# Attention with top-k, then an exact-GELU MLP: one attention item normalised inside the next item's search, and the MLP begun one slot earlier

## The chip, the cores and the metric

The kernel runs on one core of one Trainium2 chip. The metric is the device time of one execution in microseconds (us), the median of several runs. The core's engines are called PE (matrix products; PEld is its loading of weights), DVE (vector), ACT (activation functions and copies), POOL (GpSimd) and SP (which issues DMAs here). Each executes its own list of instructions in order, and they wait for each other by semaphores.

## The reference

```python
# q, k, v: (8, 8, 576, 64) float32; w_in: (512, 2048), w_out: (2048, 512), both handed over as float64
scores = scale * np.matmul(q, k.transpose(0, 1, 3, 2))
kth = np.partition(scores, -32, axis=-1)[..., -32:-31]
scores = np.where(scores >= kth, scores, -1e9)
scores = scores - np.max(scores, axis=-1, keepdims=True)
attn = np.exp(scores)
attn = attn / (np.sum(attn, axis=-1, keepdims=True) + 1e-09)
o = np.matmul(attn, v).astype(np.float32)
x = o.transpose(0, 2, 1, 3).reshape(4608, 512)
h = x @ w_in
g = 0.5 * h * (1.0 + erf(h / sqrt(2)))
out = (g @ w_out).astype(np.float32)
```

For each query the 32 largest of 576 scores are kept, the softmax is taken over them, the result multiplies v, and the rows of all heads together are the 4608 tokens of an MLP with 2048 hidden features.

## The kernel before, in words

**Items and slots.** Two heads of one batch are a pair. An item is 128 query rows of both heads of a pair, so a score tile is 128 partitions by 2 x 576. There are 144 items (a batch of 576 rows has four full row tiles per pair; the last 64 rows of two pairs share one item). The order of the items is made in the list `items`: in batch 0, items 0 to 7 are row tiles 0 and 1 of the pairs 0 to 3, items 8 to 15 are row tiles 2 and 3 of these pairs, 16 and 17 are the remainders. The scheduling is manual: the order in which the Python program issues instructions is the order in each engine's list. The main loop (L616) runs over slots n. In one slot, item n+2 gets its scores (`scores`, PE and ACT), item n its search for the 32 largest (`top_k`, DVE: four rounds of two MAX8 with three rounds of two MATCH_REPLACE8 between them, L323 and L326), item n-1 its softmax (`softmax`, ACT: a steep Prelu against the threshold at L362, and an Exp that also sums, L363), item n-2 its transposes (`transposes`: the PE transposes at L394 and L412, and ACT's copies from PSUM into the tile pt at L395 and L419), and item n-3 its product with v (`attend`, only when n-3 is the second item of a pair of row tiles: 20 PE rows at L443 for both, and a copy into xT at L448).

**Normalising.** After the softmax of item n-1, POOL adds 1e-9 to its sums (`add_small`, L355). DVE takes the reciprocal (`inverse`, L349); in `top_k` a dictionary of hooks says after which round it is issued, and before the change this is always round 3, the end of the search. Then `normalise` (L375) multiplies the two halves of the item, on DVE or POOL: with on_dve = 0 both on POOL, 1 one on each, 2 both on DVE. L660 picks this from the weight unit that the next slot will convert, since conversion keeps POOL busy. `threshold` makes the negated threshold and maximum on POOL (L338, L341) from the search's result.

**Weights.** The float64 weights are loaded as 16-bit words and converted to float32 in 16 units, one to a slot: slots 1 to 15 and 17, in the order given by `ORDER`. ACT does two steps of a unit (L174, L176) and, up to the slot before START, a third one (L178, an unsigned conversion); from slot START on the third step is POOL's (L190) and `on_pool` says so. POOL adds the parts at L193 and L194 (`weights_add`).

**The MLP** is cut into pieces in one list, `pieces`. A piece of the first layer (l1, L495) is two matmuls of 128x256 for full row tiles; a piece of the second layer (l2, L531) is one of 128x512. Eight make a block: two l1 blocks come first, then l2 and l1 blocks alternate. Two gelus (L506) on ACT are issued behind the first block, and behind the sixth piece of each l2 block. Gelu and Exp lie in different tables of ACT, so a table is loaded each time ACT turns from one to the other. A slot issues up to `left[0]` pieces spread between its attention work: 8, or 7 in the seven slots after START. A piece is issued only when its tokens are there: `attend` raises `n_tok` when a row tile is complete over all four pairs. The first 256 tokens are complete with item 7's product, the next 256 with item 15's, which is issued in slot 18. After START (`late`) the second half of the softmax is issued behind the first transposes rather than directly behind the first half. START is 2 * NP + 2 = 10 with NP = 4 pairs.

**PSUM.** The tiles of tag "tp" (q/k transposes, the scores' tail t_ps, the transposes of an item, the product o) take turns in two buffers, so each waits until ACT has copied out the tile two before it. The l1 results have two buffers of their own (tag "l1").

**SP** issues the loads of q, k, v, the weights and the stores of the output, in program order.

Of the kernel before, what the change touches and what calls it, by code (L numbers as in the profile page):

```python
# [14 lines left out]
def kernel(  # L15
# [19 lines left out]
    nc = tc.nc  # L35
# [3 lines left out]
    ALU = mybir.AluOpType  # L39
# [6 lines left out]
    NP = H // 2  # L46
# [74 lines left out]

    ORDER = [0, 1, 2, 3, 8, 9, 4, 5, 10, 11, 6, 7, 12, 13, 14, 15]
    FIRST = 1
    START = 2 * NP + 2
    WARM = 16
    words = {}
    low = const.tile([P, 1], f32, name="low")
# [52 lines left out]
    def on_pool(u):  # L180

        return SLOT_OF[u] >= START

# [23 lines left out]
    def place_of(b, row):  # L207

        if row < SM:
            return b // 2 * RING + b % 2 * (SM + 2 * TL) + row  # L210
        return b // 2 * RING + SM + b % 2 * TL + row - SM

    N = len(items)
# [30 lines left out]
    S_of, stat_of = {}, {}  # L244

    def row(i, e):
        return S_of[i][:, e * S : (e + 1) * S]
# [10 lines left out]
    def halves(t, e, step):  # L258

        return spread(t[:, e * TL :], step + (TL if e == 0 else -TL), TL)  # L260
# [47 lines left out]
    def top_k(i, hooks):  # L308


        stat_of[i] = st = {
            "top": work.tile([P, 2, TOPK], f32, tag="top", name="top"),
            "neg": work.tile([P, 2, 2], f32, tag="neg", name="neg"),
            "bias": work.tile([P, 2], f32, tag="bias", name="bias"),
            "den": work.tile([P, 2], f32, tag="den", name="den"),
            "rden": work.tile([P, 2], f32, tag="rden", name="rden"),
        }
        cur = [row(i, e) for e in range(2)]
        rest = work.tile([P, 2, S], f32, tag="rest", bufs=1, name="rest")
        n_op = 0  # L320
        for r in range(TOPK // 8):
            for e in range(2):
                nc.vector.max(st["top"][:, e, 8 * r : 8 * r + 8], cur[e])  # L323
            if r < TOPK // 8 - 1:
                for e in range(2):
                    nc.vector.match_replace(  # L326
                        rest[:, e], st["top"][:, e, 8 * r : 8 * r + 8], cur[e], LOWEST
                    )
                cur = [rest[:, e] for e in range(2)]
            if r in hooks:  # L330
                hooks.pop(r)()
# [13 lines left out]
    def inverse(i):  # L345
        if i < 0 or i >= N:
            return
        st = stat_of[i]
        nc.vector.reciprocal(st["rden"], st["den"])  # L349

    def add_small(i):
        if i < 0 or i >= N:
            return
        st = stat_of[i]
        nc.gpsimd.tensor_scalar(st["den"], st["den"], 1e-9, None, op0=ALU.add)  # L355
# [12 lines left out]
    def normalise(i, on_dve):  # L368

        if i < 0 or i >= N:  # L370
            return
        st = stat_of[i]
        for e in range(2):
            s = row(i, e)
            (nc.vector if e >= 2 - on_dve else nc.gpsimd).tensor_scalar(  # L375
                s, s, st["rden"][:, e : e + 1], None, op0=ALU.mult
            )
# [5 lines left out]
    def transposes(i):  # L383

        if i < 0 or i >= N:
            return []
        t, s = items[i][1], S_of.pop(i)

        def tails():
            tp = ps.tile([P, 512], f32, tag="tp", name="tp_t")  # L390
            if t < NM:
                if t % 2 == 0:
                    pt_now[0] = work.tile([P, 2 * NM + 1, 2 * P], f32, tag="pt", name="pt")
                nc.tensor.transpose(tp[:, 0:P], s[:, SM : S + TL], ident)  # L394
                nc.scalar.copy(out=pt_now[0][:, 2 * NM, t % 2 * P : (t % 2 + 1) * P], in_=tp[:, 0:P])  # L395
            else:
                pt_now[0] = ptt
                for r in range(2):
                    nc.tensor.transpose(
                        tp[0:TL, r * P : (r + 1) * P], s[:, r * S + SM : (r + 1) * S], ident  # L400
                    )
                for e in range(2):
                    c = slice(e * TL, (e + 1) * TL)
                    nc.scalar.copy(
                        out=halves(ptt[c, 0, NM, :], e, NJ * P), in_=halves(tp[0:TL, 0 : 2 * P], e, P)
                    )

        def main(e):
            tp = ps.tile([P, 512], f32, tag="tp", name="tp")
            first = e * (S + TL if t < NM else S)  # L410
            for j in range(NM):
                nc.tensor.transpose(  # L412
                    tp[:, j * P : (j + 1) * P], s[:, first + j * P : first + (j + 1) * P], ident
                )
            if t < NM:
                dst = pt_now[0][:, e * NM : (e + 1) * NM, t % 2 * P : (t % 2 + 1) * P]
            else:
                dst = ptt[:, e, 0:NM, :]
            nc.scalar.copy(out=dst, in_=tp.rearrange("p (j n) -> p j n", j=NM))  # L419

        return [tails] + [lambda e=e: main(e) for e in range(2)]
# [3 lines left out]
    def attend(i):  # L425

        if i < 0 or i >= N:
            return False
        pair, t = items[i]
        b, at = divmod(pair, NP)  # L430
        if t < NM and t % 2 == 0:
            return False
        pt = pt_now[0]
        o = ps.tile([P, 512], f32, tag="tp", name="o")
        n, row = (2 * P, (t - 1) * P) if t < NM else (TL, SM)
        tok = place_of(b, row)
        assert read[0] >= tok + n - RING
        c = slice(tok % RING, tok % RING + n)
        if t < NM:
            vt = raw_of("v", pair)  # L440
            for j in range(NJ):
                for e in range(2):
                    nc.tensor.matmul(  # L443
                        o[e * D : (e + 1) * D, 0:n], lhsT=vt[:, j, e, :],
                        rhs=pt[:, e * NM + j if j < NM else 2 * NM, :],
                        start=(j == 0), stop=(j == NJ - 1),
                    )
            nc.scalar.copy(out=xT[:, at, c], in_=o[:, 0:n])  # L448
        else:
            for r in range(2):  # L450
                vt = raw_of("v", pair + r)
                for j in range(NJ):
                    for e in range(2):
                        nc.tensor.matmul(  # L454
                            o[e * D : (e + 1) * D, r * TL : (r + 1) * TL], lhsT=vt[:, j, e, :],
                            rhs=pt[:, r, j, half(r, e)], start=(j == 0), stop=(j == NJ - 1),
                        )
            nc.scalar.copy(
                out=xT[:, at : at + 2, c],
                in_=o[:, 0 : 2 * TL].rearrange("p (r n) -> p r n", r=2),  # L460
            )

        if t == (NM if b % 2 == 0 else NM - 1):
            for r in range(2 if t == NM else 1):
                load("v", pair + r + NP + 1)
        if at == (NP - 1 if t < NM else NP - 2):
            assert n_tok[0] == tok
            n_tok[0] = tok + n
        return True
# [146 lines left out]
    for n in range(ahead):  # L616

        left[0] = 7 if START < n < START + 2 * NP else 8
        weights_add(unit_in(n))
        scores(n + 2)  # L620
        product = attend(n - 3)
        late = n > START
        mlp(1)
        tr = transposes(n - 2)
        if product and n > START and done[0] < len(pieces) and pieces[done[0]][0] > ready[0]:

            for piece in tr[:1]:
                piece()
            tr, ready[0] = tr[1:], n_tok[0]
        softmax(n - 1, 0)  # L630
        mlp(1)
        if not late:
            softmax(n - 1, 1)
        mlp(1)
        prep = prep_in.pop(n, [])
        if len(prep) > 1 and len(tr) == 3:
            tr, prep = tr[:1] + prep[:1] + tr[1:], prep[1:]
        for piece in tr[:-1]:
            piece()
            ready[0] = n_tok[0]  # L640
            mlp(1)
        ready[0] = n_tok[0]
        if late:
            softmax(n - 1, 1)
        add_small(n - 1)
        for piece in tr[-1:] + prep:
            piece()
            mlp(1)

        run_gelus()  # L650
        mlp(left[0])
        run_gelus()
        if n < N:
            top_k(n, {3: lambda: inverse(n - 1)})
        else:
            inverse(n - 1)
        threshold(n)
        u = unit_in(n + 1)

        normalise(n - 1, 0 if u not in words else 2 if on_pool(u) else 1)  # L660

        weights_size(unit_in(n + 1))
        if n >= FIRST:
            load_weights(n + 2)
        if n <= NP:
            load("v", n)
# [38 lines left out]
```

## Time and profile before

| | |
|---|---|
| median of 5 runs | 1655.5 us (1654.88 to 1658.2) |
| profiled execution, its own time | 1658.2 us |
| its span | 1656.4 us |
| PE busy | 1596.7 us (96%) |
| DVE busy | 1419.7 us (86%) |
| ACT busy | 1185.1 us (72%) |
| POOL busy | 651.6 us (39%) |

The span is the time from the first to the last instruction that the profile records; the run's own time has 1.8 us more. Time in the profile is counted from the span's start. DVE begins the search of slot 8 at 94.72 us, of slot 9 at 105.06, of slot 10 at 115.83 and of slot 18 at 210.89; the last search ends before 1603. A row of the profile in order of time gives the start, the length, the engine, the line, the operation with the tile that it writes and those that it reads, how many such instructions follow on each other, and in brackets how long the engine had been idle and what ended that. The count of PE rows is of hardware matmuls: a float32 matmul of the program is two. "PEclk" is the granted clock of PE as a share of full speed.

### The profile page before, as it was taken

The numbers are of one execution on the slowest core, as the hardware profiler recorded it, in microseconds if no ns is written. First come the engines' busy times: TensorE is split into PE (matmuls) and PEld (weight loads), VectorE is DVE, ScalarE is ACT, GpSimd is POOL, SyncE is SP. The second block draws the span as 40 slices with busy tenths as digits, with TensorE's granted clock in tenths as the row PEclk, the third lists the DMA queues.
The fourth block names the chain that finished last, engine by engine and source line by source line (L and its number), as shares of the span: only waits on it lengthen the run. The fifth ranks groups of instructions, "written<-read, shape, count | busy, mean of one in ns | idle before, by whom it ended". The sixth has DMA issues, their size and how long they took to land.

```text
span 1656.4 us, 25056 instructions
## 1 busy us (share of the span) xinstructions
PE 1596.7 (96%) x8832; PEld 1081.4 (65%) x8832; DVE 1419.7 (86%) x3049; ACT 1185.1 (72%) x2131; POOL 651.6 (39%) x756
## 2 busy tenths in 40 slices
PE   6669899999999999999999999999999999999999
PEld 4446566766666667676666667676666666666665
DVE  7998889999999898998999888998889898999800
ACT  6888767777777777777777777777777777777720
POOL 3677643333333333333333333333333333333300
PEclk7669999999999999999999999999999999999999
DMA  6423210011100111011110111001110001000000
GB/s 165 138 99 98 87 42 1 14 29 29 49 1 22 32 30 31 1 28 36 29 28 1 42 29 43 1 14 28 44 35 1 27 15 32 4 14 3 5 13 13
DMA packets 126621, 56.14 MB, mean 34 GB/s; under 512 B 117760, under 2 KB 117792, under 8 KB 126496
## 3 DMA queue, kind: packets, MB, share of 16 engines
q1 hardware_dynamic: 125376, 54.25, 12.2%
q8 instruction: 70, 1.15, 0.3%
q14 instruction: 55, 0.45, 0.1%
q10 hardware_dynamic: 1056, 0.26, 0.1%
q0 software_dynamic: 64, 0.03, 0.0%
HBM read 45.08 MB, written 9.44 MB: 33 GB/s over the span
## 4 chain that ended last, share of the span: by engine, by line
PE 90%; DVE 6%; ACT 3%; POOL 0%; issue 0%; ACTq 0%; DVEq 0%; POOLq 0%
PE h_ps L495 30%; PE y_ps L531 30%; PE o L443 8%; PE s_ps L276 7%; PE tp L412 7%; DVE top L323 3%; DVE rest L326 2%; PE tp_qk L231 2%; PE t_ps L272 2%; PE o L454 1%; PE s_ps L297 1%; PE tp_t L394 1%; ACT s L363 1%; ACT s L362 1%; POOL s L375 0%; PE warm L595 0%
## 5 line engine op out<-in xcount | busy, mean ns | idle before, releaser
L323 DVE MAX8 top<-rest 128x8 f32<-128x576 f32 x864 | 610.1, 748 | 0.0
L495 PE MATMUL h_ps<-xT,w_in_sb 128*128 128x256 f32 (+1 forms) x2560 | 554.8, 362 | 3.8 <-ACT g L506 3.8
L531 PE MATMUL y_ps<-w_out_sb,g 128*128 128x512 f32 x1152 | 549.4, 599 | 0.0
L495 PEld LDWEIGHTS h_ps<-xT,w_in_sb 128*128 128x128 f32 x2560 | 429.4, 191 | 67.1 <-issue 19.6
L375 POOL TENSOR_SCALAR s<-s,rden 128x576 f32<-128x576 f32 x266 | 456.6, 1726 | 0.8 <-issue 0.4
L326 DVE MATCH_REPLACE8 rest<-top,rest 128x576 f32<-128x576 f32 x576 | 423.8, 744 | 0.0
L355 POOL TENSOR_SCALAR den<-den 128x2 f32<-128x2 f32 x144 | 32.1, 223 | 837.6 <-ACT s L363 837.1
L531 PEld LDWEIGHTS y_ps<-w_out_sb,g 128*128 128x128 f32 x1152 | 195.0, 190 | 166.9 <-issue 165.1
L280 ACT ACTIVATE s<-s_ps 128x1024 f32<-128x1024 f32 x128 | 131.6, 1028 | 168.3 <-PE s_ps L276 149.6
L363 ACT ACTIVATE s<-s,bias 128x576 f32<-128x576 f32 x288 | 223.7, 777 | 13.3 <-ACT s L362 0.7
L362 ACT ACTIVATE s<-s,neg 128x576 f32<-128x576 f32 x288 | 224.0, 778 | 0.3 <-POOL neg L338 0.2
L412 PEld LDWEIGHTS tp<-ident,s 128*128 128x128 f32 x1152 | 145.5, 144 | 116.7 <-issue 59.1
L419 ACT COPY pt<-tp 128x512 f32<-128x512 f32 x256 | 147.4, 576 | 102.6 <-PE tp L412 102.6
L326 DVE MATCH_REPLACE8 rest<-top,s 128x576 f32<-128x576 f32 x288 | 211.8, 743 | 0.0
L412 PE MATMUL tp<-ident,s 128*128 128x128 f32 x1152 | 178.7, 279 | 28.2 <-ACT pt L395 23.1
L323 DVE MAX8 top<-s 128x8 f32<-128x576 f32 x288 | 201.9, 743 | 3.9 <-ACT s L281 3.9
L443 PE MATMUL o<-pt,raw_v 128*64 128x256 f32 x1280 | 156.4, 392 | 0.0
L276 PE MATMUL s_ps<-qk 64*128 64x256 f32 x1024 | 154.6, 423 | 0.7 <-ACT s L280 0.7
L349 DVE RECIPROCAL rden<-den 128x2 f32<-128x2 f32 x144 | 23.2, 161 | 144.8 <-POOL den L355 144.5
L443 PEld LDWEIGHTS o<-pt,raw_v 128*64 128x64 f32 x1280 | 88.1, 140 | 66.5 <-issue 23.3
L276 PEld LDWEIGHTS s_ps<-qk 64*128 64x128 f32 x1024 | 93.1, 196 | 24.2 <-issue 2.2
L506 ACT ACTIVATE g<-h_ps 128x512 f32<-128x512 f32 x144 | 78.6, 595 | 34.0 <-PE h_ps L495 33.2
(66 smaller groups left out, 1092.1 us busy)
## 6 DMA issues: line engine op xcount, KB each, us to landing
raw_q<-in_q_dram SPq DMA_DIRECT2D x64, 128.0 KB, 2.3
raw_v<-in_v_dram SPq DMA_DIRECT2D x64, 128.0 KB, 2.4
out_dram<-y SPq DMA_DIRECT2D x32, 256.0 KB, 2.2
w_out_sb<-in_moe_w_in_dram SPq DMA_DIRECT2D x16, 511.8 KB, 4.8
raw_k<-in_k_dram SPq DMA_DIRECT2D x62, 128.0 KB, 2.4
w_out_sb<-in_moe_w_out_dram SPq DMA_DIRECT2D x10, 511.8 KB, 4.0
words<-in_moe_w_out_dram SPq DMA_DIRECT2D x6, 511.8 KB, 4.2
raw_q<-in_q_dram SPq DMA_DIRECT2D x64, 16.0 KB, 2.1
```

What stands on the lines that cost most here:

```text
L276: nc.tensor.matmul(s_ps[:, e, c * 256 : (c + 1) * 256], lhsT=lhsT[rows, :], rhs=qk[rows, KT + c * 256 : KT + (c + 1) * 256], start=True, s ...
L280: nc.scalar.activation(spread(s, S + TL, SM), s_ps, func=AF.Copy, scale=scale)
L323: nc.vector.max(st["top"][:, e, 8 * r : 8 * r + 8], cur[e])
L326: nc.vector.match_replace(rest[:, e], st["top"][:, e, 8 * r : 8 * r + 8], cur[e], LOWEST)
L362: nc.scalar.activation(s, s, func=AF.Prelu, bias=st["neg"][:, e, 1:2], scale=1.0, alpha=STEEP)
L363: nc.scalar.activation(s, s, func=AF.Exp, bias=st["bias"][:, e : e + 1], scale=1.0, accum_out=st["den"][:, e : e + 1],)
L375: (nc.vector if e >= 2 - on_dve else nc.gpsimd).tensor_scalar(s, s, st["rden"][:, e : e + 1], None, op0=ALU.mult)
L412: nc.tensor.transpose(tp[:, j * P : (j + 1) * P], s[:, first + j * P : first + (j + 1) * P], ident)
L419: nc.scalar.copy(out=dst, in_=tp.rearrange("p (j n) -> p j n", j=NM))
L443: nc.tensor.matmul(o[e * D : (e + 1) * D, 0:n], lhsT=vt[:, j, e, :], rhs=pt[:, e * NM + j if j < NM else 2 * NM, :], start=(j == 0), stop= ...
L495: nc.tensor.matmul(h_tile(u)[:, i, :], lhsT=w_in_sb[:, ko, f * P : (f + 1) * P], rhs=xT[:, ko, c0 : c0 + n], start=(ko == 0), stop=(ko == ...
L531: nc.tensor.matmul(y_of[sub], lhsT=g_of[u][:, i, sub * P : (sub + 1) * P], rhs=w_out_sb[:, f, :], start=(f == 0), stop=(f == FT - 1),)
```

## The change

The item HASTE = 7 is handled one slot sooner than the other items. In slot 8, a hook after round 1 of item 8's search (instead of round 3) lets DVE add the 1e-9, take the reciprocal and normalise both halves of item 7; POOL's `add_small` and the usual `normalise` are left out for it. Its transposes are issued at the end of slot 8, behind those of item 6, and not in slot 9; its product is issued in slot 9 and not in slot 10. START becomes 9, which moves three things with it: the slots with 7 pieces are 10 to 16, the `late` order of the softmax begins in slot 10, and the weight unit of slot 9 has its unsigned conversion on POOL.

```diff
     FIRST = 1
-    START = 2 * NP + 2
+    START = 2 * NP + 1
+    HASTE = 2 * NP - 1
...
         scores(n + 2)
-        product = attend(n - 3)
+
+        product = attend(HASTE) if n - 2 == HASTE else n - 3 != HASTE and attend(n - 3)
         late = n > START
         mlp(1)
-        tr = transposes(n - 2)
+        tr = transposes(n - 2) if n - 2 != HASTE else []
...
-        add_small(n - 1)
+        if n - 1 != HASTE:
+            add_small(n - 1)
...
-        if n < N:
+        if n - 1 == HASTE:
+
+            def hasty():
+                st = stat_of[HASTE]
+                nc.vector.tensor_scalar(st["den"], st["den"], 1e-9, None, op0=ALU.add)
+                inverse(HASTE)
+                normalise(HASTE, 2)
+
+            top_k(n, {1: hasty})
+            for piece in transposes(HASTE):
+                piece()
+        elif n < N:
             top_k(n, {3: lambda: inverse(n - 1)})
         else:
             inverse(n - 1)
         threshold(n)
         u = unit_in(n + 1)
 
-        normalise(n - 1, 0 if u not in words else 2 if on_pool(u) else 1)
+        if n - 1 != HASTE:
+            normalise(n - 1, 0 if u not in words else 2 if on_pool(u) else 1)
```

## The prediction

> **What bounds the kernel now.** I read first how the execution splits into stretches (stretch, length, then busy time and instructions of PE, PEld, DVE, ACT, POOL; clock; DMA).
>
> ```profile
> 0.00:215.00 215.00, 160.23 (x828) 105.74 (x829) 191.42 (x411) 169.88 (x279) 136.36 (x123) 0.83 0.38 113
> 215.00:1603.00 1388.00, 1387.90 (x7845) 945.38 (x7845) 1228.33 (x2640) 1008.90 (x1841) 515.29 (x633) 1.00 0.09 22
> 1603.00:1656.40 53.40, 48.57 (x161) 30.32 (x160) 0.00 (x0) 6.33 (x11) 0.00 (x0) 0.99 0.05 20
> ```
>
> From 215 us on PE has no idle time (1387.90 of 1388.00) at clock 1.00. Before that it is idle for 55 us and its clock averages 0.83. So the end is the moment at which PE enters the full stretch, plus fixed work, as long as the work after that moment is the same. Next, PE's order of time around that moment (start, length, operation, idle before):
>
> ```profile
> 119.89 0.33 PE L394 MATMUL tp_t<-ident,s 128*128 128x128 f32 x1
> 120.05 1.03 PE L495 MATMUL h_ps<-xT,w_in_sb 128*128 128x256 f32 x4
> ...
> 214.97 0.34 PE L399 MATMUL tp_t<-ident,s 128*64 128x128 f32 x1 [1.41 <-POOL s L375]
> 215.11 3.58 PE L495 MATMUL h_ps<-xT,w_in_sb 128*128 128x256 f32 x8
> 218.52 0.60 PE L412 MATMUL tp<-ident,s 128*128 128x128 f32 x4
> ```
>
> The MLP starts at 120.05 in slot 10. Slot 18 waits at 214.97 for POOL's normalisation of item 16, and its first two pieces take 3.4 us, twice the warm price (a piece starts 0.86 us after the one before: 1.03 with its tail). Last, who waits for whom from 94 to 216 (total, times, longest):
>
> ```profile
> POOL den L355 <- ACT s L363: 19.1, 6, 7.5
> ...
> DVE rden L349 <- POOL den L355: 10.5, 5, 3.3
> ...
> PE tp L412 <- ACT pt L395: 8.8, 5, 2.7
> ```
>
> DVE waits 10.5 us in five slots for the sums, which POOL gets late from ACT; PE waits for ACT's evacuations. Slots 10 to 17 hang on ACT and PE in turn, DVE has slack.
>
> **What stays the same.** The first 256 tokens hold 56 pieces: l1 blocks 0, 2, 4, 6 and l2 blocks 0, 2, 4, of eight each. The next l1 block needs tokens that item 15's product makes in slot 18, with or without the change. Before, slots 10 to 17 issue 8+7x6+6 = 56 pieces; after, slots 9 to 16 do, and slot 17 issues none. From slot 18 on the order of every engine is the same; SP's order is the same throughout, and item 7's transposes and product issue no DMA. So eight pieces are not gained outright: slot 9 fills and slot 17 empties, and the gain is what slot 17 shrinks by, and what the shift does between.
>
> **Slot 8, the hook on DVE.** It issues add, reciprocal and two scalings, and takes a reciprocal and one scaling from the slot's end.
>
> ```profile
> 100.27 1.41 DVE L323 MAX8 top<-rest 128x8 f32<-128x576 f32 x2
> 101.11 0.19 ACT L363 ACTIVATION_READ_ACCUMULATOR s<-s,bias 128x1 f32 x1
> ...
> 104.37 0.15 DVE L349 RECIPROCAL rden<-den 128x2 f32<-128x2 f32 x1
> ```
>
> DVE gets to the hook at 100.27, the sum is there at 101.30: a wait of 1.1. Then the add (no row; DVE's 128x2 reciprocal, 0.15, is nearest; between 0.06 and POOL's 0.22) 0.2, the reciprocal with hand-over 0.28 (later slots), two scalings 0.95: done at 102.9, 2.5 behind. The slot's end gives back 0.7, so the search of slot 9 starts at 106.85, not 105.06. Queued behind are only later searches, covered by those 10.5 us; without that cover it costs 1.8. POOL loses an add and a 1.73 us scaling and gets the 3.1 us unsigned conversion of slot 9's weight unit; ACT loses that unit's 1.11 us copy. POOL's next sum, item 8's, is then ready at about 115.9, before DVE's reciprocal at 116.5.
> The Trainium skill ("SBUF — State Buffer", Who interferes with whom) speaks against the hook: a DVE scaling in a 2-port mode and a GpSimd operation lock each other out for a whole instruction. Rows here agree: POOL's L341 takes 0.35 us beside DVE's scaling and 0.20 without. By the rule the hook could wait out POOL's 2.40 us L194; but that ends at 101.43, before the scalings at 101.9. By the row 0, by the rule at most 2.4, still inside DVE's slack; I take 0.
>
> **Slots 8 and 9 on PE.** Item 7's transposes follow at 102.95, cold, with two turns of PSUM: to 105.2. Scores(11) cold (0.57+2.08): 107.85. The product is 20 rows at 0.212 cold (4.25) or 0.1155 warm (2.31). The clock returned at 95.6 and 119.5, after 3.3 and 6.5 us of unbroken work. The Trainium skill ("TensorE: Matmul & The Clock Gate", Part 1) says why they differ: full clock comes after one busy window of some 3.4 us, and the window runs free. The two moments are 23.9 us apart, seven such windows. By the longer row alone the clock would come at about 112 (product to 112.1); by the rule between 106.4 and 112, in this profile's phase at 109.3 (7 rows cold, product to 110.8). I take the rule's; the difference is 1.3 us. Two q/k transposes 0.22 and eight pieces at 0.86: PE leaves slot 9 at 118.0. Slot 10 before:
>
> ```profile
> 129.93 0.39 PE L272 MATMUL t_ps<-qk 128*128 128x128 f32 x2
> ```
>
> The first eight pieces are thus done 11.9 us sooner, and ACT's second gelu, which waits for them, moves from 130.12 to 118.1.
>
> **Slots 10 to 16**, walked with the start-to-start times of the rows. ACT: weights 2.4, scores 1.06, first softmax half 1.75 (2.93 with table load), small evacuation 0.14, large 0.48, second half 1.6, large 0.46, q/k 0.48, gelu pair with load 2.27. PE: scores 1.38, product 2.31, piece 0.86, small transpose 0.11, four 0.44. DVE: a search 9.65, with reciprocal and two scalings 10.77. PSUM of the transposes has two buffers, so each third tile waits for ACT. PE's slots then start at 118.0, 127.9, 136.8, 148.4, 157.3, 173.1, 182.5 and slot 17 at 194.0: 76.0 us, where slots 11 to 17 before took 77.9 (129.93 to 207.87). The products fall in other slots than before (12, 14, 16 with slot 14's gelu pair in mid-slot), so lengths differ; slot 14 is the longest with 15.8:
>
> ```profile
> 182.90 1.10 PE L495 MATMUL h_ps<-xT,w_in_sb 128*128 128x256 f32 x4 [2.67 <-ACT g L506]
> ```
>
> this stall comes again there, at about 165. Weights are in time: each piece uses units converted at least one slot earlier.
>
> **Slots 17 and 18.** Without pieces, ACT sets slot 17: gelu pair 194.4 to 196.7, the last unit's weights to 199.2, scores to 200.3, softmax(16) with reload to 205.45. POOL's add, DVE's reciprocal and POOL's two scalings (3.43) end at 209.8. PE works unbroken from 203.5 (last transposes, scores(20), product of item 15), by the same windows warm from 208.3, product done at 209.9, small transposes at 210.3; two warm pieces 1.73: four-transpose group at 212.0 instead of 218.52. Gain 6.5. If the clock comes one window later, at 211.7: 4.7. Middle 5.6; the walk leaves out some 0.1 us of hand-over in each of eight slots, 0.8. **Gain 4.8 us.** The sum is made in a profiled execution of 1656.4 span and 1658.2 in time (1.8 around it), the highest of the five runs; I take the difference off the median: 1655.5 - 4.8 = **1650.7**.
>
> **Rivals.** *Given back in slot 17* (0.22): the walk's seven ACT-bound slots lose another 0.3 to 0.5 each and slot 17's chain of loads, weights and softmax gets longer, so 12 us of lead at slot 9 shrink to 2: about 1653.5. For it: one more slot in which PE idles five microseconds and cools. Against: DVE has slack, and slot 17's chain has rows for all its parts.
> *Half clock all through slot 9* (0.09), the other side: product +1.5, eight pieces +6.9, together 8.4: 1650.7+8.4 = 1659.1. It decides from some 16 us of cold work beyond 109.3 (each costs half; 4.8+3.3 must be lost). Against: unbroken work never waited over 6.5 us for the clock here.
> *Nothing moves* (0.03): item 7's transposes wait for something unseen and the MLP still starts near 120: 1655.5.
>
> **Numbers.** About 0.2% (3.3 us) can be told from no change. The forecast has 0.66. Faster 0.66, same 0.25, slower 0.09. Most it could be: DVE's searches without any wait end slot 17 at 201.8 instead of 210.83, 9 us. Range: 1647.0 (half a microsecond short of that) to 1655.7 (all of the second case, none of the third); the forecast's own is 1647.5 to 1652.2.
>
> **What would show it.** First MLP matmul near 111, a second gelu near 118; DVE's hook waiting about 1 us; a slot without MLP and PE idle about 5 us near 196; PE unbroken from about 210, four transposes of item 16 at about 212. Wrong if the clock stays at 0.5 past 113, if softmax(16) ends after 208, or if PE idles after slot 18.

## The result, and the profile after

The changed kernel takes 1652.19 us (median of 25 runs, 1649.79 to 1653.05) against 1655.54 us before (45 runs, 1654.17 to 1658.2): a ratio of 0.9978, 95% interval 0.9972 to 0.9983. That is 3.35 us, or 0.2%, faster; the forecast was 4.8 us. The profiled execution of the changed kernel has a span of 1650.4 us and a time of 1652.21, within 0.02 us of its median; that of before, 1658.2, was the slowest of these 45 runs.

In the stretches of the changed kernel (the columns as in the prediction), PE is full again from the moment it begins slot 18's pieces of the MLP, and the work after that is the same length:

```profile
0.00:210.80 210.80, 156.30 (x828) 104.26 (x829) 192.87 (x412) 170.05 (x279) 137.08 (x122) 0.83 0.39 115
210.80:1598.00 1387.20, 1386.22 (x7845) 944.21 (x7844) 1228.24 (x2640) 1008.42 (x1842) 515.27 (x633) 1.00 0.09 22
```

1387.2 us with PE busy for 1386.2 of them. From item 16's first four transposes in slot 18 to the end of the span it is 1437.87 us here and 1437.88 before (1437.87 to 1437.94 in all fourteen profiles of this document): nothing is gained or lost behind slot 18. PE in order of time, the first MLP pieces, the stall of slot 14, and slots 17 and 18:

```profile
107.29 3.07 PE L444 MATMUL o<-pt,raw_v 128*64 128x256 f32 x20
...
110.56 7.07 PE L496 MATMUL h_ps<-xT,w_in_sb 128*128 128x256 f32 x32
117.47 0.39 PE L273 MATMUL t_ps<-qk 128*128 128x128 f32 x2
...
167.94 1.10 PE L496 MATMUL h_ps<-xT,w_in_sb 128*128 128x256 f32 x4 [2.66 <-ACT g L507]
...
196.34 0.33 PE L395 MATMUL tp_t<-ident,s 128*128 128x128 f32 x1
201.24 1.12 PE L413 MATMUL tp<-ident,s 128*128 128x128 f32 x4 [4.57 <-ACT s L304]
204.30 1.12 PE L413 MATMUL tp<-ident,s 128*128 128x128 f32 x4 [1.94 <-ACT pt L396]
205.20 0.64 PE L273 MATMUL t_ps<-qk 128*128 128x128 f32 x2
...
210.67 0.30 PE L400 MATMUL tp_t<-ident,s 128*64 128x128 f32 x1 [0.29 <-POOL s L376]
210.80 1.89 PE L496 MATMUL h_ps<-xT,w_in_sb 128*128 128x256 f32 x8
212.53 0.60 PE L413 MATMUL tp<-ident,s 128*128 128x128 f32 x4
```

The MLP starts at 110.56 and slot 9 ends at 117.47. Slot 17 has no pieces: PE is idle for 4.57 and 1.94 us there, because the PSUM buffers of its transposes wait for ACT's copies, and it starts slot 18 at 205.20. The last line, item 16's first four transposes, is the mark of the prediction: 212.53 instead of 218.52. In the table of waits from 94 to 211 (total us, count, longest), DVE's wait for the sums has gone from 10.5 to 5.1 us:

```profile
DVE rden L350 <- POOL den L356: 5.1, 4, 2.9
```

### The profile page after: what moved, and what is told of

It reads as the page before. It is cut to its first block, busy times and chain, and to the rows that moved or that the text cites. A ratio compares the mean times of both kernels' runs of the same rounds, so it can differ in the third digit from the quotient of the medians.

```text
span 1650.4 us, 25054 instructions
## 1 busy us (share of the span) xinstructions
PE 1591.0 (96%) x8832; PEld 1078.8 (65%) x8832; DVE 1421.1 (86%) x3051; ACT 1184.0 (72%) x2130; POOL 652.4 (40%) x755
## 4 chain that ended last, share of the span: by engine, by line
PE 90%; DVE 6%; ACT 2%; POOL 1%; issue 0%; DVEq 0%; POOLq 0%; ACTq 0%
PE h_ps L496 30%; PE y_ps L532 30%; PE o L444 8%; PE s_ps L277 7%; PE tp L413 7%; DVE top L324 3%; DVE rest L327 3%; PE tp_qk L232 2%; PE t_ps L273 2%; PE o L455 1%; PE s_ps L298 1%; PE tp_t L395 1%; POOL s L376 0%; ACT s L364 0%; PE warm L596 0%
```

## The experiments

All twelve were timed beside the kernel before (its median there 1655.56 to 1655.58). The changed kernel was not timed again beside them; where a run is compared with its 1652.19 us, that rests on the medians of before, which agree within 0.04 us. As profiles begin at slightly different moments, times are also compared from one anchor, DVE's reciprocal at the end of slot 7, to item 16's first four transposes in slot 18: from 94.03 it is 124.49 us in the first profile of before, from 93.77 it is 118.76 in the changed kernel, 5.73 less.

### Before, once more

No edit.

> The kernel before, unchanged, for a second profile and a second set of times. Theory (the first profile was taken in an execution whose clock came late in slots 10 and 18, so it is 2.7 us above the median): span about 1653.7, first full MLP stretch near 212 to 213 instead of 215.11, with a shorter stretch of half clock in slot 10 or slot 18. Rival (the difference lies in the fixed part after slot 18): the stretch begins at 215 again, and the rest is shorter.

1655.05 us, as before (ratio 0.9999, 0.9990 to 1.0008); the profiled execution took 1654.76, its span 1653.0, 0.3 us under the median of these runs. DVE in order of time, and below it PE:

```profile
136.88 0.17 DVE L349 RECIPROCAL rden<-den 128x2 f32<-128x2 f32 x1 [0.79 <-POOL den L355]
...
186.50 0.17 DVE L349 RECIPROCAL rden<-den 128x2 f32<-128x2 f32 x1 [4.01 <-POOL den L355]
```

```profile
114.04 3.13 PE L443 MATMUL o<-pt,raw_v 128*64 128x256 f32 x20
...
127.14 0.38 PE L272 MATMUL t_ps<-qk 128*128 128x128 f32 x2
...
206.11 0.38 PE L272 MATMUL t_ps<-qk 128*128 128x128 f32 x2
...
213.22 0.30 PE L399 MATMUL tp_t<-ident,s 128*64 128x128 f32 x1 [1.41 <-POOL s L375]
213.36 1.89 PE L495 MATMUL h_ps<-xT,w_in_sb 128*128 128x256 f32 x8
215.09 0.60 PE L412 MATMUL tp<-ident,s 128*128 128x128 f32 x4
```

From anchor to mark it is 121.31 us, 3.2 less than in the first profile, with the same instructions. Item 7's product takes 3.13 rather than 4.25 us, so DVE's wait in slot 11 is 0.79 and not 3.32 (2.5 less); the two pieces of slot 18 are at full clock, 1.89 and not 3.58 (1.7 less); against that DVE waits 4.01 and not 2.98 in slot 15 (1.0 more), where PE was for a while at half clock. The theory holds: the difference between the two executions is when the clock returned. Against this profile the changed kernel's gain is 2.55 us.

How little of the early start is left can be read from PE's slots. The first eight pieces are done 9.67 us sooner (at 127.14, the end of slot 10, against 117.47, the end of slot 9). The seven slots with the other pieces take 77.47 us instead of 78.97. But slot 17 now comes on top as a slot without pieces, and it takes 10.26 us, more than the 7.64 it took with six of them: ACT's pair of gelus and the two table loads around it (at 195.39 and 201.93) now lie in it. So slot 18 starts only 0.91 us sooner (205.20 against 206.11).

What the mark waits for is another chain, and it is the same in both kernels: DVE's reciprocal in slot 17, then POOL's two scalings of item 16. In this profile of before, and below it in the changed kernel:

```profile
209.07 0.15 DVE L349 RECIPROCAL rden<-den 128x2 f32<-128x2 f32 x1
209.73 3.43 POOL L375 TENSOR_SCALAR s<-s,rden 128x576 f32<-128x576 f32 x2
```

```profile
206.65 0.17 DVE L350 RECIPROCAL rden<-den 128x2 f32<-128x2 f32 x1 [1.02 <-POOL den L356]
207.18 3.43 POOL L376 TENSOR_SCALAR s<-s,rden 128x576 f32<-128x576 f32 x2
```

POOL's scalings start 2.55 us sooner, which is the gain at the mark. DVE does one search after the other, so the moment of this reciprocal is the time of the searches plus what DVE waits for sums. These waits in slots 9 to 17 add up to 8.98 us here and to 5.07 in the changed kernel, 3.9 less; the rest of DVE's time since the anchor is 106.31 and 107.81, 1.5 more, about what the hook of slot 8 costs (it puts the search of slot 9 at 106.45 instead of 104.81). The shift pays because the sums come sooner to DVE.

### Item early, the MLP held until slot 10

```diff
-        left[0] = 7 if START < n < START + 2 * NP else 8
+        left[0] = 0 if n <= 2 * NP + 1 else 7 if 2 * NP + 2 < n < 4 * NP + 2 else 8
```

> Item 7 is normalised and multiplied early as in the changed kernel, START is 9, but the MLP is held until slot 10 with 8 pieces there and 7 in slots 11 to 17. Theory (the MLP's eight pieces a slot sooner are what pays): about the time before, within 1.5 us (1654 to 1657). Rival (what pays is that item 7's product and transposes are out of the way when slot 10's pieces come): 2 to 4 us faster than before, about 1652.5.

1653.55 us, ratio 0.9985 (0.9976 to 0.9993): 2.0 us faster than before, so the rival, at the edge of its range. But the edit held the pieces less than was meant. PE's list is not tied to DVE's slots:

```profile
109.70 2.86 PE L496 MATMUL h_ps<-xT,w_in_sb 128*128 128x256 f32 x12
116.30 0.30 PE L395 MATMUL tp_t<-ident,s 128*128 128x128 f32 x1 [3.75 <-DVE s L376]
```

Three of slot 10's eight pieces run at 109.70, because nothing of item 7 stands before them any more; PE then waits 3.75 us for DVE's scaling of item 8. The rows agree with the rival: item 7's transposes and product have left slot 10 on PE, and the pieces that follow come sooner wherever they are written. It is not shown apart from the early pieces, and the profile is the fastest of the eleven runs (1651.62). The interval overlaps that of the changed kernel, so how much of 3.35 us the early slot itself brings is not settled.

### START alone

```diff
-    START = 2 * NP + 2
+    START = 2 * NP + 1
```
(in the kernel before)

> The kernel before with START = 9 alone: slots 10 to 16 take 7 pieces, the softmax order turns in slot 10, slot 9's unit is converted on POOL; item 7 is untouched, so the MLP still starts in slot 10. Theory (START's side effects are worth nothing): 1655.5, within 1 us. Rival (the fewer pieces in slot 10 or the third conversion step on POOL carry part of the gain): 1 to 3 us faster than before.

1660.5 us, ratio 1.0031 (1.0019 to 1.0044): 5 us slower; both theories missed. With seven pieces in slot 10 the eighth, which releases the first pair of gelus, is in slot 11, and so are they, in the middle of a softmax. ACT in order of time there, and below it PE:

```profile
127.76 1.28 ACT L506 ACT_TABLE_LOAD   x1
129.06 1.08 ACT L506 ACTIVATE g<-h_ps 128x512 f32<-128x512 f32 x2
133.74 0.27 ACT L395 COPY pt<-tp_t 128x128 f32<-128x128 f32 x1 [3.60 <-PE tp_t L394]
```

```profile
129.71 3.78 PE L495 MATMUL h_ps<-xT,w_in_sb 128*128 128x256 f32 x8 [3.75 <-ACT g L506]
```

PE waits 3.75 us for the gelus, its two pieces then take 3.78 us, which is half clock, and ACT in turn waits 3.60 us for PE. DVE's waits for sums add up to 13.0 us in this profile. START's three effects were not taken apart in this kernel; that the place of the gelus costs the 5 us is read from these rows.

### Item early, START left at 10

```diff
-    START = 2 * NP + 1
+    START = 2 * NP + 2
```
(in the changed kernel)

> The changed kernel with START left at 10: item 7 early, the MLP still starts in slot 9 because its tokens are there, slots 9 and 10 take 8 pieces, 11 to 15 take 7, slot 16 takes 5. Theory (START's side effects are worth nothing, the end is set by slot 17's chain on ACT): as the changed kernel, 1652.2 within 1 us. Rival (START carries part of the gain): 1 to 3 us slower than the changed kernel, 1653.5 to 1655.

1655.32 us, ratio 1.0000 (0.9991 to 1.0009): the whole gain is gone, as the rival said, and a little more than it said; DVE's waits add up to 8.55 us. Each half of the change alone gives nothing or a loss: START has to be the slot in which the MLP really starts. The next three runs take START's three effects back one at a time.

```diff
-        late = n > START
+        late = n > START + 1
```

> The changed kernel with only the order of the softmax as if START were 10: in slot 10 both halves of softmax(9) go ahead of item 8's evacuations. Theory (slot 10 on PE waits 1.3 us longer for ACT's evacuation, and DVE gets its sums sooner by as much, so it is mostly covered): 1652.2 to 1653.2. Rival: it carries the 3 us, 1655.

1654.36 us, ratio 0.9993 (0.9984 to 1.0002), 2.2 us above the changed kernel: more than the theory allowed, less than the rival's whole. PE in slot 10:

```profile
126.67 0.65 PE L413 MATMUL tp<-ident,s 128*128 128x128 f32 x4 [2.45 <-ACT pt L396]
...
129.33 0.38 PE L273 MATMUL t_ps<-qk 128*128 128x128 f32 x2
```

The evacuation of item 8's small transpose stands behind both halves of softmax(9), PE waits 2.45 us instead of 0.88, and the next slot starts at 129.33 instead of 127.52. Nothing later gives this back: DVE's waits add up to 7.33 us instead of 5.07.

```diff
-        left[0] = 7 if START < n < START + 2 * NP else 8
+        left[0] = 7 if START + 1 < n < START + 1 + 2 * NP else 8
```

> The changed kernel with only the count of pieces as if START were 10: eight in slots 9 and 10, seven in 11 to 15, five in 16. Theory (START's worth is the place of the gelus: the second and third pair now fall elsewhere between the softmax halves, and slot 10 gets longer): most of the 3.1 us that the variant with START = 10 lost, about 1654.5. Rival (the softmax order in slot 10 is what counts): within 0.7 us of the changed kernel.

1652.66 us, ratio 0.9986 (0.9977 to 0.9995): 0.5 us above the changed kernel, not to be told from it; the theory's 1654.5 fell.

```diff
-        return SLOT_OF[u] >= START
+        return SLOT_OF[u] > START
```

> The changed kernel with only slot 9's weight unit converted by ACT as before (1.11 us more on ACT ahead of scores(11), 3.1 us less on POOL). Theory (ACT then waits for item 7's product anyway, 1.62 us idle in the changed profile): within 0.5 us of the changed kernel, 1652.2. Rival: 1 us slower, 1653.3.

1652.65 us, ratio 0.9981 (0.9972 to 0.9990): within 0.5 us, as the theory said. By the medians the three parts, 2.2, 0.5 and 0.5 us, add up to the 3.1 us lost with START at 10, and the softmax order in slot 10 carries most; each is uncertain by some 1.5 us. The kernel before with this softmax order alone was not run, so whether the order would pay without the early item stays open.

### Fillers against half clock

A helper issues products of the identity into an unused PSUM buffer, so PE stays busy where it would be idle. In the kernel before:

```diff
+    def fill(m):
+        t = ps.tile([P, 512], f32, tag="l1", name="fill")
+        for _ in range(m):
+            nc.tensor.matmul(t[:, 0:P], lhsT=ident, rhs=ident, start=True, stop=True)
...
+        if n == 18:
+            fill(12)
         tr = transposes(n - 2)
...
+        if n in (7, 8, 9):
+            fill(8)
         for piece in tr[-1:] + prep:
```

> The kernel before with idle-time fillers on PE (products of the identity into an unused PSUM buffer, result not read): eight in each of slots 7, 8 and 9 ahead of the last transposes, twelve in slot 18 ahead of item 16's. Theory (half clock in slots 9, 10 and 18 lies on the path to the full stretch and, by its shifting phase, makes the scatter of the times): clock back to 1.00 by slot 10's product, 1.5 to 3 us faster than before (1652.5 to 1654), scatter smaller. Rival (the clock there is covered by ACT): 1655.5 within 1 us.

1653.94 us (1652.97 to 1654.10), ratio 0.9989 (0.9980 to 0.9998): 1.6 us faster than before by doing more, and these eleven runs span 1.1 us where seventeen of before span 2.9. The product of slot 10 takes 2.38 us, all at full clock, and DVE's wait in slot 11 is 0.26 us. The theory holds in its time: half clock in slots 9 to 18 is on the path. That its phase makes the scatter fits, but is not all of it: the anchor itself, in slot 7, lies between 92.63 and 94.03 us in the fourteen profiles. In the changed kernel:

```diff
         tr = transposes(n - 2) if n - 2 != HASTE else []
+        if n == 17:
+            tr = tr[:1] + [lambda: fill(24)] + tr[1:]
...
+        if n in (7, 8, 17):
+            fill(8)
         for piece in tr[-1:] + prep:
```

> The changed kernel with the same fillers in slots 7 and 8, and 24 + 8 of them in slot 17, where PE is idle. Theory (from slot 10 on DVE has only 0.27 us of slack and slot 18 waits for POOL's scalings, so clock gained in slots 9 and 17 is covered): 1651.7, 0 to 1 us faster than the changed kernel. Rival (half clock is what still costs): 2 to 3 us faster.

1650.49 us (1650.32 to 1651.39), ratio 0.9972 (0.9962 to 0.9983): by the medians 1.7 us below the changed kernel, between the two theories; the intervals overlap. The gain was not all covered: the wait of DVE in slot 14 is 1.50 instead of 2.90 us. What is left is POOL's scaling of item 16:

```profile
207.42 0.30 PE L400 MATMUL tp_t<-ident,s 128*64 128x128 f32 x1
208.94 0.30 PE L400 MATMUL tp_t<-ident,s 128*64 128x128 f32 x1 [1.23 <-POOL s L376]
```

With both scalings of item 16 on DVE as well:

```diff
-            normalise(n - 1, 0 if u not in words else 2 if on_pool(u) else 1)
+            normalise(n - 1, 2 if n == 17 else 0 if u not in words else 2 if on_pool(u) else 1)
```

> As the previous one, with both scalings of item 16 (slot 17) on DVE rather than POOL: 0.95 instead of 3.43 us. Theory (slot 17's end is bound by softmax(16), POOL's scalings and the half clock of PE together): 1.5 to 2.5 us faster than the changed kernel, about 1650.3. Rival (the wait for DVE's search takes over): within 0.7 us of the previous one.

1649.01 us, ratio 0.9966 (0.9953 to 0.9978): another 1.5 us by the medians, the 1.23 us of the line above and a little more. That is 3.2 us below the changed kernel, more than the theory's 1.5 to 2.5, and the rival's 0.7 is passed too, though this step by itself is within the intervals. The five runs span 2.2 us, fillers or not.

### The second pair of gelus at a slot's end

```diff
-        left[0] = 7 if START < n < START + 2 * NP else 8
+        left[0] = 9 if n == 13 else 7 if START < n < START + 2 * NP else 8
```
(in the changed kernel)

> The changed kernel with nine pieces in slot 13 instead of seven, so that the second pair of gelus issues at that slot's end and not in the middle of slot 14; slot 16 then has four pieces. Theory (slot 14's 2.66 us of PE idle time and DVE's wait of 2.90 come from the two table loads amid the softmax, and are not covered): 2 to 3 us faster than the changed kernel, about 1649.7. Rival (slot 17's chain on ACT sets the end whatever slot 14 does): within 0.7 us of the changed kernel.

1648.72 us, ratio 0.9958 (0.9944 to 0.9971): 3.5 us below the changed kernel, more than expected, with intervals that just do not meet. PE in slot 14:

```profile
166.25 0.60 PE L232 MATMUL tp_qk<-ident,raw_k 128*128 128x128 f32 x4
166.69 1.03 PE L496 MATMUL h_ps<-xT,w_in_sb 128*128 128x256 f32 x4
```

Where the changed kernel waits 2.66 us between these two, PE goes on, and DVE's wait there is 0.47 us instead of 2.90; its wait of 0.88 in slot 16, which now has two pieces fewer, is gone as well. The pair of table loads is the same in both (gelu's at 157.01 and the softmax's at 163.93, against 165.91 and 170.80); only its place differs.

### All of them

Fillers, item 16 on DVE and nine pieces in slot 13 together.

> The changed kernel with fillers in slots 7, 8 and 17, item 16 scaled by DVE, and nine pieces in slot 13. Theory (the gelu place gains some 3.5 us in slots 14 to 16, the fillers and DVE's scaling 3.2 us in slots 9 and 17, in different places, so they add): 1645.5 to 1646.5. Rival (DVE's searches become the bound and swallow half): 1647 to 1648.5.

1645.07 us (1644.45 to 1645.48), ratio 0.9938 (0.9925 to 0.9950): 10.5 us faster than before and 7.1 faster than the changed kernel, somewhat more than the sum of the parts. DVE's reciprocals of slots 9 to 17:

```profile
115.18 0.15 DVE L350 RECIPROCAL rden<-den 128x2 f32<-128x2 f32 x1
125.95 0.15 DVE L350 RECIPROCAL rden<-den 128x2 f32<-128x2 f32 x1
136.72 0.15 DVE L350 RECIPROCAL rden<-den 128x2 f32<-128x2 f32 x1
147.49 0.15 DVE L350 RECIPROCAL rden<-den 128x2 f32<-128x2 f32 x1
158.26 0.15 DVE L350 RECIPROCAL rden<-den 128x2 f32<-128x2 f32 x1
169.04 0.14 DVE L350 RECIPROCAL rden<-den 128x2 f32<-128x2 f32 x1
179.81 0.14 DVE L350 RECIPROCAL rden<-den 128x2 f32<-128x2 f32 x1
189.51 0.14 DVE L350 RECIPROCAL rden<-den 128x2 f32<-128x2 f32 x1
200.31 0.17 DVE L350 RECIPROCAL rden<-den 128x2 f32<-128x2 f32 x1
```

10.77 to 10.80 us from each to the next where two scalings lie between, 9.70 from slot 15 to slot 16 where POOL scales: not one wait for the sums. In these slots DVE's searches are now the bound, as the rival of this run said, but they swallowed nothing of the gains. The prediction's limit for this chain, slot 17's end at 201.8, is 107.8 us from the anchor; here it is 107.5.

## Why the prediction was right or wrong

**The frame was right in its end.** The end moved with the mark in slot 18; behind the mark the same 1437.9 us follow in every profile, and slot 9 filled as slot 17 emptied. Two of its steps were not right. Slot 17 did not shrink, it grew from 7.64 to 10.26 us. And "DVE has slack" does not hold at the end of the chain: in slot 17 of the kernel before DVE's reciprocal comes without a wait, and POOL's scaling and the mark hang on it. The slack lies in the five slots before, and it is these waits that became shorter.

**The walk was close, in profile against profile.** It put PE's slots 10 to 17 at 118.0, 127.9, 136.8, 148.4, 157.3, 173.1, 182.5 and 194.0; they start at 117.47, 127.52, 136.44, 148.19, 157.32, 173.48, 183.18 and 194.94. The mark was expected at 212.0 (warm) and came at 212.53, 6.0 us earlier than in the first profile (5.7 from the anchor) against 6.5 worked out. The 76.0 us of slots 10 to 16 measure 77.5, 1.5 more where 0.8 was allowed for hand-overs.

**The term that was mis-sized** is the last one, "I take the difference off the median". The prediction noted that the profiled execution was the highest of the five runs and still subtracted a difference formed in it. In that execution the clock had come back late in slot 10, 6.5 us into unbroken work, and slot 18 was cold too; the second profile, near the median, is 3.2 us shorter from anchor to mark. From anchor to mark the gain against it is 2.55 us, against the first one 5.73; the medians, 3.35, lie between. The forecast of 4.8 came as near as it did by some luck: 1.7 us had been taken off the 6.5 for a later window of the clock and for hand-overs, and this hid part of the 2.7 us by which the profiled execution lay above the median.

**The hook** cost what was said, in the changed profile for another reason. The search went on 2.33 us late (102.34 after 100.01) against 2.5. The wait was put down to ACT's sum, and a lock-out by POOL to the two scalings, at 0. In the changed profile the sum was there in time, and it was the add that waited, for POOL's L195 (below). In eight of the ten profiles with the hook DVE did wait for the sum first, 0.17 to 1.06 us, and in all ten the search went on 2.25 to 2.40 us after the round before it. The slack of DVE covered the delay as forecast, but barely: the wait for the sum in slot 10 is down to 0.27 us.

**START was under-priced.** The prediction priced the moved conversion, and gave the softmax order and the counts of pieces no term of their own; the walk had the order in, since it put slot 11 at 127.9 (127.52 measured; 129.33 with the old order). The runs show 2.2 us for the order alone and 5 us lost for START without the early item.

**The clock rule** was the right choice over the longer row: the product of item 7 took 3.07 us (107.29 to 110.29), where the rule gave 2.95 and the row alone 4.25. Of the rule's range, 106.4 to 112, the clock met nearly the moment that was taken (about 108.7 for 109.3), and that is luck, since the window's phase in another execution was not known. One of the two rows behind it was misread: before 95.6 PE had worked without a gap since 91.45, 4.2 us and not 3.3. The 23.9 us between the two moments do not depend on that.

**The rivals.** "Given back in slot 17" is largely what happened: 9.67 us of lead shrink to 0.91 at slot 18's start. The other 1.64 us at the mark are slot 18's: it waits 0.29 us for POOL's scaling instead of 3.06, and loses 1.1 of that by starting at half clock. The measured 1652.19 lies at the very edge of the forecast's own range, 1652.2. Half clock through slot 9 did not occur: PEclk was back to 1.00 by 109. (The figure given for it, 1659.1, lay outside the stated range, which ended at 1655.7.)

## What to carry to other kernels

A difference worked out in one profiled execution holds for that execution: where it is at the slow end of the runs, look for what in it is luck (here the phase of PE's clock) before the difference is taken off the median. A piece of work moved a slot ahead does not bring its lead to the end: here 9.67 us of it became 0.91, as the slot that it emptied had a chain of its own on ACT. So look first at that chain, and at what the end waits for; here it was DVE's waits for sums that had to shrink. And where an engine changes tables, the place of the pair of loads within the slot was worth as much here as the whole change.

## What was not expected of the hardware

A DVE operation on 128x2 elements, 0.17 us long by itself, took 1.17 us because POOL was in a long tensor operation. The hook's add, POOL's L195 and the sum (ACT) in order of time in the changed profile, and below it the add and the sum with the item early and START at 10:

```profile
98.75 2.39 POOL L195 TENSOR_TENSOR w_in_sb<-w_in_sb,w_out_sb 128x1024 int32<-128x1024 int32 x1
...
99.43 0.19 ACT L364 ACTIVATION_READ_ACCUMULATOR s<-s,bias 128x1 f32 x1
100.01 1.17 DVE L660 TENSOR_SCALAR den<-den 128x2 f32<-128x2 f32 x1
```

```profile
101.08 0.19 ACT L364 ACTIVATION_READ_ACCUMULATOR s<-s,bias 128x1 f32 x1
101.30 0.17 DVE L660 TENSOR_SCALAR den<-den 128x2 f32<-128x2 f32 x1 [0.97 <-ACT s L364]
```

In the first, the sum was ready at 99.62; the add begins at 100.01 and ends at 101.18, 0.04 us after POOL at 101.14. In six more profiles with the hook it ends 0.02 to 0.04 us after L195 too, 0.23 to 1.17 us long by how much of L195 was left when it began; in the remaining three, where it began within 0.1 us of L195's end, it takes 0.17. Not every DVE operation is held: a MATCH_REPLACE8 of 128x576 at 99.35, also beside L195, takes its usual 0.74. This agrees with the exclusive lock of the Trainium skill ("SBUF — State Buffer", Who interferes with whom), which the prediction had applied to the large scalings only; the small add was held for the whole rest of POOL's operation. That the add runs in a 2-port mode is taken from this and not shown, and a version without the overlap was not run.

Filling PE's idle time with useless products made both kernels faster by 1.6 to 1.7 us at the median. Their runs span 1.1 us each, eleven and seven of them, but the five with item 16 on DVE span 2.2, so the narrower scatter is not sure.
